# Routing attention with a PReLU FFN on one core: two more pairs of heads in cluster order

## The chip, the cores and the metric

The kernel runs on one core of a Trainium2 chip. The metric is the device time in microseconds of one execution, taken as the median of several runs. TensorE (PE in the profile) multiplies, with its weight loads on a row of their own (PEld); VectorE (DVE), ScalarE (ACT) and GpSimd (POOL) work elementwise; SyncE (SP) only issues transfers, and POOL issues those whose rows are scattered by a list of indices.

## The reference

```python
# q, k, v: (4 batches, 8 heads, 768 tokens, 64); centroids: (8 heads, 16 clusters, 64)
q_assign = argmax(einsum('bhsd,hcd->bhsc', normed(q), normed(centroids)))
k_assign = argmax(einsum('bhsd,hcd->bhsc', normed(k), normed(centroids)))
mask   = q_assign[:, :, :, None] == k_assign[:, :, None, :]
scores = where(mask, q @ k.T / 8, -1e9)
x      = softmax(scores) @ v             # -> (3072 tokens, 512)
h      = x @ w_in                        # 512 -> 2048
g      = maximum(h, 0) + alpha * minimum(h, 0)
out    = g @ w_out                       # 2048 -> 512
```

A query sees only the keys of its own cluster. All products are computed in fp32; the FFN's weights arrive as 64-bit floats and are converted on the chip.

## The kernel before

**Work.** Two heads make a pair `n`; batch `b` has pairs `4b` to `4b+3`, 16 in all. 768 tokens are six tiles of 128, and a half is three tiles (384 columns). In a *full* pair, every half of the queries meets all six chunks of keys: `score` (L757) makes 12 products of 384 columns, ScalarE takes the exponential (L775, L778), VectorE multiplies by the mask (L798), adds up the chunks (L808), transposes and reduces them to row sums (L827, L835), and `weigh` (L893) multiplies by v. `total` (L848) adds the sums across partitions, and `normalise` (L993) writes into `xTs[b, half]`, the FFN's input.

**Pairs in cluster order.** Pairs from `NO` on, 12 to 15, all of batch 3, are treated in another way. Some steps ahead their tokens are ordered by cluster. `load` brings q and k, `order_features` (L562) transposes them into two new tiles, `order_sims` (L573) finds the clusters, `order_counts`, `order_begins` (L598), `order_ranks` and `order_rows` work out each token's row. `order_stage` (L645) loads 256 tokens of q, k and v of one head into one of two stage tiles, three transfers on SP; `order_scatter` (L663) writes 128 rows to a scratch tensor in HBM by an indirect transfer on POOL. A pair has 6 stages and 24 scatters. `order_load` (L669) reads the ordered rows back. Once ordered, a chunk of keys can only match queries in its own tile and the two beside it, so `window(c)` gives each chunk two or three tiles of queries and not six: all of a pair's scores are 12 products, of 256 or 384 columns, and `weigh_near` (L926) has 16, of 128 to 384 columns. `add_near` (L818, L821) adds what lies near. Afterwards the rows go back into their order: `normalise_near` (L932) makes an output tile, `to_rows` (L955) transposes it in two groups of three, ScalarE copies each group to `rows` (L958), `put_back` (L963) scatters it with 12 indirect transfers on POOL, `fetch_back` (L975) reads it with four transfers, and `turn_back` (L985) transposes it into `xTs`, both halves at once.

**Steps and slots.** Everything is emitted in one order written out by hand. `steps` lists three steps for each half of a full pair and three for each pair in cluster order; `UB` = 12 steps make a block. For the first three batches the list runs over halves, pairs and steps, and for batch 3 over pairs and steps:

```python
steps = [(b * NCH + hp, half, s)
         for b in range(WHOLE) for half in range(2)
         for hp in range(NCH) for s in range(SB)]
steps += [(n, None, s) for n in range(NO, NP) for s in range(SB)]
```

From step 24 on (`TOGETHER`) a step has five slots; the first step of a half scores all chunks, and leaves two slots. `later(k, piece)` emits a piece k slots on. `ORDERS` gives the steps at which the four orderings begin; the rest of their times follows from it. `sorting` is a queue of the stages and scatters, from which one piece is emitted in each slot.

**FFN as filler.** The FFN of one half (28 pieces: 16 of four hidden products, L1017; 12 of four output products, L1035) is put in the queue `ffn` when its input is complete, and fed between the attention of the next block, evenly over its slots. `kept(block)` says how many pieces stay in the queue at the end of a block: 4 at the end of the last but one, 12 at the end of the last. These 12 cover the way back of the last pair's rows. The FFN of batch 3 is done at the very end with seven products in place of eight (`last_pieces`, L1195 and L1251).

**Buffers.** `inp` has four tiles for loads, ordered loads, output tiles and fetched rows; `xpool` has two for `xTs`, and one more, `xmore`, holds the second half of batch 3; `ps_m` (`misc`) is one PSUM bank for all small products and the transposes.

Of the kernel before, what the change touches and what calls it, by code (L numbers as in the profile page):

```python
# [19 lines left out]
P = 128  # L20
# [3 lines left out]
def kernel(  # L24
# [79 lines left out]
    pairs = [(b, hp) for b in range(B) for hp in range(NCH)]  # L104
    NO = WHOLE * NCH
    NP = len(pairs)
# [455 lines left out]
    def order_features(n, w):  # L562
        us[n, w] = inp.tile([P, 2, NJ, D], FP32, name="qk").rearrange("p h j d -> p (h j d)")
        nc.vector.transpose(out=us[n, w],
                            in_=raw_qk.pop((n, w)).rearrange("p h j d -> p (h j d)"))

# [11 lines left out]
    def order_counts(n, ps):  # L578

        top, first, pieces = argmax(ps, exact=True)  # L580
        member = sorts["ordp"].tile([P, HS], BF16, name="mine")
        pieces.append(lambda: nc.vector.transpose(
            out=member, in_=top.rearrange("p t c -> p (t c)")))

        def scan():
            count = asg.tile([P, HS], FP32, name="simT")
            nc.vector.tensor_tensor_scan(count, member, member, 0.0, ALU.add, ALU.max)
            us[n] = member, count
        pieces.append(scan)
        for i, piece in enumerate(pieces):  # L590

            later(i if i < len(pieces) - 2 else i + 2, piece) if i else piece()

    def order_begins(n):
# [17 lines left out]
    def order_rows(n, begin, count):  # L612
        ordp, order = sorts["ordp"], sorts["order"]
        by_token = ordp.tile([P, NX, 2, NC], FP32, name="by_token")
        nc.vector.transpose(out=by_token.rearrange("p x h c -> p (x h c)"), in_=count)
        rank = ordp.tile([P, NX, 2], FP32, name="rank")
        nc.vector.tensor_reduce(out=rank, in_=by_token, axis=AX.X, op=ALU.add)
        off = order.tile([P, NX, 2], I32, name="off")
        nc.vector.tensor_scalar(out=off, in0=rank, scalar1=0.0, scalar2=float(2 * S - 1),
                                op0=ALU.max, op1=ALU.min)  # L620
        ranks[n] = off
        whole = tc.dram_tile([2 * 2 * S, P], FP32, name=f"scratch{n}")
        scratch[n] = whole, dram_disjoint_views(whole, 2 * NX)
# [79 lines left out]
    def order_queries(n, h):  # L703
# [225 lines left out]
    def normalise_near(n):  # L929
        outT = inp.tile([P, 2, NJ, D], FP32, name="qk").rearrange("p h j d -> p (h j d)")  # L930
        for side in range(2):
# [5 lines left out]
        found = orders.pop(n)  # L937
        place = sorts["order"].tile([P, 2, NJ], I32, name="place")
        nc.vector.tensor_scalar(out=place, in0=found[:, :, :, 0], scalar1=0, scalar2=S - 1,
                                op0=ALU.max, op1=ALU.min)  # L940
        rows = sorts["byrow"].tile([P, NJ, P], FP32, name="rows")

        starts = (6, 9)
        for i in range(2):
            later(starts[i], lambda i=i: to_rows(outT, rows, i))
            for x in range(NJ):
                later(starts[i] + 2 + x // 2,
                      lambda i=i, x=x: put_back(to, place, rows, i * NJ + x))
        later(starts[1] + 2 + HJ, lambda: fetch_back(n, whole))

    def to_rows(outT, rows, i):

        ps = misc()
        for j in range(HJ):
# [3 lines left out]
        later(1, lambda: nc.scalar.copy(  # L958
            rows[:, i * HJ:(i + 1) * HJ].rearrange("p j d -> p (j d)"), ps[:, 0:HS]))

    def put_back(to, place, rows, i):
# [3 lines left out]
            out_offset=bass.IndirectOffsetOnAxis(ap=place[:, h, j:j + 1], axis=0),  # L965
            in_=rows[:, j, h * D:(h + 1) * D], in_offset=None, element_offset=h * S * D)

    def fetch_back(n, whole):
# [11 lines left out]
        def turn_back():  # L980
            for half in range(2):
                if (b, half) not in xTs:
                    pool = sorts["xmore"] if half else xpool
                    xTs[b, half] = pool.tile([P, NCH, HS], FP32, name="xT")
                nc.vector.transpose(out=xTs[b, half][:, hp, :],  # L985
                                    in_=raw[:, half * HS:(half + 1) * HS])
        later(4 if n == NP - 1 else 9, turn_back)

    def normalise(n, half):
        b, hp = pairs[n]  # L990
        if (b, half) not in xTs:
            xTs[b, half] = xpool.tile([P, NCH, HS], FP32, name="xT")
        nc.vector.tensor_tensor(out=xTs[b, half][:, hp, :],  # L993
                                in0=pos.pop((n, half))[:, 0:HS],
# [98 lines left out]
    def last_pieces():  # L1093
# [195 lines left out]
        def room_for_y():  # L1289
            late.popleft()()  # L1290
            t = xpool.tile([P, NCH, HS], FP32, name="xT").rearrange("p c q -> p (c q)")
            ys.extend(ypool.tile([P, DM], FP32, name="y") for _ in range(HJ))
# [25 lines left out]

    ORDERS = [27, 33, 51, 57]
    prep_at, load_at = {}, {}  # L1320
    for (n, half), u in start_of.items():
        def at(step, slot, piece):
            prep_at.setdefault((step, slot), []).append(piece)
        if half is None:
            t = ORDERS[n - NO]
            load_at.setdefault(t, []).append(lambda n=n: load(n))
            for i in range(2):
                at(t + 2, 2 + 2 * i, lambda n=n, i=i: order_features(n, i))
# [47 lines left out]
    def feed_block(u):  # L1376
        n, half, _ = steps[u - 1]
        if u == NS:
# [4 lines left out]
            return  # L1383
        for i in (range(2) if half is None else (half,)):
            ffn.extend(ffn_pieces(pairs[n][0], i))

    def kept(block):


        return {NS // UB - 2: 4, NS // UB - 1: 12}.get(block, 0)  # L1390

# [55 lines left out]
    for u in range(TOGETHER, NS + 1):  # L1447
# [4 lines left out]
        if s == 0 or u == NS:  # L1452
# [17 lines left out]
            else:  # L1470
                normalise(*prior)
            if u % UB == 0:
                feed_block(u)
                whole = len(ffn) - kept(u // UB)
            if u == NS:
# [21 lines left out]
        else:  # L1497
            slots = range(SLOTS)
        if u == ORDERS[0] - 2:
            order_constants()  # L1500
        for i in slots:
            tick()
            if s == 0:
                prepare(u, FIRST + i - 3)
            at_slot = (u % UB) // SB * FREE + (s * SLOTS + i - 3)
            left = UB // SB * FREE - 1 - at_slot
            pieces = len(ffn) - kept(u // UB) + -whole * left // (UB // SB * FREE)
# [231 lines left out]
```

## Time and profile before

| | us |
|---|---|
| median of 3 runs (963.44 to 963.97) | 963.72 |
| the profiled execution, its own time | 968.97 |
| its span, first to last instruction | 967.2 |
| TensorE busy | 946.1 |
| VectorE busy | 683.5 |
| ScalarE busy | 260.0 |
| POOL busy | 213.2 |

The granted TensorE clock is 1.000 over the whole span. "Busy" of an engine is the time in which at least one of its instructions runs. A group of instructions is named by line, engine and operation, with the tiles it writes and reads, the number of records (an fp32 product leaves two), and the mean length; overlapping instructions count once in the busy time, so that busy time over count is less than the mean.

### The profile page before, as it was taken

What the parts mean: (1) busy time and instruction counts of PE and PEld (TensorE: products, weight loads), DVE (VectorE), ACT (ScalarE), POOL (GpSimd) and SP (SyncE); (2) the same over time, 40 slices, a digit from 0 to 9 for tenths busy, and PEclk for the clock granted to TensorE, in tenths of its full rate; (3) what the DMA queues carried; (4) which work ended last, traced back from release to release, by engine and by line L of the source; (5) the groups of instructions that cost most, each with busy time, mean ns of one, the idle gap of its engine ahead of it and who ended that gap; (6) DMA issues with size and microseconds to landing.
All of it is one profiled execution on the core that took longest, in us unless ns stands there. A gap on an engine that the chain in (4) does not pass through costs nothing.

```text
span 967.2 us, 11202 instructions
## 1 busy us (share of the span) xinstructions
PE 946.1 (98%) x4059; PEld 502.8 (52%) x4059; DVE 683.5 (71%) x1241; ACT 260.0 (27%) x474; POOL 213.2 (22%) x249
## 2 busy tenths in 40 slices
PE   8999999999999999999999999999998999999997
PEld 5534444445454454544545445454454454556886
DVE  5897788798587776977868777678888735598200
ACT  5764533323121231222312223222222210121000
POOL 1432222110000645401000065550043541000000
PEclk9999999999999999999999999999999999999999
DMA  8433666053200463416020031450621112000000
GB/s 290 141 113 102 143 136 118 17 114 88 55 1 22 127 134 70 87 28 123 1 33 1 25 89 50 94 103 11 88 49 30 33 32 56 1 1 0 21 24 25
DMA packets 175583, 64.67 MB, mean 67 GB/s; under 512 B 161360, under 2 KB 165152, under 8 KB 175520
## 3 DMA queue, kind: packets, MB, share of 16 engines
q1 hardware_dynamic: 170064, 55.62, 25.6%
q0 software_dynamic: 4608, 7.87, 2.5%
q8 instruction: 34, 0.56, 0.2%
q10 hardware_dynamic: 848, 0.39, 0.2%
q14 instruction: 29, 0.24, 0.1%
HBM read 45.15 MB, written 18.35 MB: 66 GB/s over the span
## 4 chain that ended last, share of the span: by engine, by line
PE 92%; DVE 5%; issue 1%; ACT 1%; POOL 0%; DVEq 0%; ACTq 0%; POOLq 0%
PE fps L1035 25%; PE fps L1017 25%; PE vps L893 9%; PE sps L757 8%; PE sps L1251 4%; PE sps L1195 4%; PE fps L757 3%; PE vps L1251 2%; PE vps L1195 2%; PE fps L1251 1%; PE fps L1195 1%; PE mps L381 1%; PE mps L926 1%; PE vps L926 1%; PE sps L766 1%
## 5 line engine op out<-in xcount | busy, mean ns | idle before, releaser
L1017 PE MATMUL fps<-xT,w_in_sb 128*128 128x384 f32 x768 | 259.2, 491 | 0.0
L1035 PE MATMUL fps<-w_out_sb,gT 128*128 128x512 f32 x576 | 256.0, 597 | 1.1 <-DVE gT L1009 1.1
L1017 PEld LDWEIGHTS fps<-xT,w_in_sb 128*128 128x128 f32 x768 | 142.3, 190 | 103.9 <-ACT more L778 4.4
L663 POOL DMA_INDIRECT scratch<-stage,off x96 | 102.0, 1063 | 324.8 <-DMA stage<-in_v_dram 269.7
L1035 PEld LDWEIGHTS fps<-w_out_sb,gT 128*128 128x128 f32 x576 | 106.9, 190 | 127.2 <-issue 117.9
L1023 ACT COPY gT<-fps 128x384 f32<-128x384 f32 x96 | 45.9, 478 | 225.0 <-PE fps L1017 212.5
L798 DVE SCALAR_TENSOR_TENSOR more<-aq,key,more 128x384 f32<-128x384 bf16 (+1 forms) x136 | 74.5, 606 | 35.1 <-ACT more L778 20.0
L757 PE MATMUL sps<-qkT 64*128 64x384 f32 (+1 forms) x512 | 97.4, 494 | 0.1
L1009 DVE SCALAR_TENSOR_TENSOR gT<-gT,alpha 128x384 f32<-128x384 f32 x96 | 61.3, 646 | 33.2 <-ACT gT L1023 24.0
L778 ACT ACTIVATE E<-sps 128x768 f32<-128x768 f32 (+1 forms) x81 | 61.0, 801 | 73.2 <-PE sps L766 38.4
L963 POOL DMA_INDIRECT back<-rows,place x48 | 47.7, 994 | 105.1 <-ACT rows L958 91.7
L757 PEld LDWEIGHTS sps<-qkT 64*128 64x128 f32 x512 | 46.3, 186 | 45.0 <-issue 18.1
L798 DVE SCALAR_TENSOR_TENSOR E<-aq,key,E 128x384 f32<-128x384 bf16 (+1 forms) x104 | 56.6, 601 | 17.2 <-ACT E L778 11.3
L893 PE MATMUL vps<-E,vt 128*64 128x384 f32 x356 | 65.7, 494 | 1.5 <-DVE xT L993 1.5
L808 DVE TENSOR_TENSOR acc<-acc,E 128x768 f32<-128x768 f32 x47 | 44.9, 955 | 14.9 <-ACT E L778 13.6
L778 ACT ACTIVATE more<-sps 128x768 f32<-128x768 f32 (+1 forms) x47 | 35.6, 796 | 49.6 <-PE fps L1035 21.6
L893 PEld LDWEIGHTS vps<-E,vt 128*64 128x64 f32 x356 | 23.0, 136 | 33.4 <-issue 31.0
L271 POOL TENSOR_TENSOR w_in_sb<-w_in_sb,power 128x512 f32<-128x512 f32 x16 | 24.3, 1520 | 71.2 <-DVE w_in_sb L268 71.2
L893 PE MATMUL vps<-more,vt 128*64 128x384 f32 x220 | 38.8, 491 | 0.0
L1041 ACT COPY y<-fps 128x512 f32<-128x512 f32 x18 | 10.5, 586 | 100.8 <-PE fps L1035 81.6
L757 PE MATMUL fps<-qkT 64*128 64x384 f32 x160 | 34.9, 508 | 0.6 <-ACT more L775 0.6
L271 POOL TENSOR_TENSOR w_out_sb<-w_out_sb,power 128x512 f32<-128x512 f32 x16 | 22.5, 1410 | 55.8 <-DVE w_out_sb L268 55.8
(282 smaller groups left out, 1074.4 us busy)
## 6 DMA issues: line engine op xcount, KB each, us to landing
raw<-in_moe_w_in_dram SPq DMA_DIRECT2D x16, 512.0 KB
raw<-in_moe_w_out_dram SPq DMA_DIRECT2D x16, 512.0 KB
out_dram<-y SPq DMA_DIRECT2D x21, 256.0 KB
vt<-in_v_dram SPq DMA_DIRECT2D x12, 384.0 KB
qk<-in_q_dram SPq DMA_DIRECT2D x48, 96.0 KB
qk<-in_k_dram SPq DMA_DIRECT2D x48, 96.0 KB
w_in_kept<-w_in_sb SPq DMA_DIRECT2D x8, 512.0 KB
qk<-scratch SPq DMA_DIRECT2D x32, 96.0 KB
```

What stands on the lines that cost most here:

```text
L271: nc.gpsimd.tensor_tensor(out=dst, in0=dst, in1=power[0].bitcast(FP32), op=ALU.mult)
L663: nc.gpsimd.indirect_dma_start(out=scratch[n][1][h * NX + xx], out_offset=bass.IndirectOffsetOnAxis(ap=ranks[n][:, xx, h:h + 1], axis=0), ...
L757: nc.tensor.matmul(out=bank(ps, h, m), lhsT=qkT[r:r + D, S + c * P:S + (c + 1) * P], rhs=qkT[r:r + D, tokens], start=True, stop=not early_ ...
L778: nc.scalar.activation(out=E[:, :, 0:m], in_=ps[:, :, 0:m], func=AF.Exp, scale=SCALE)
L798: nc.vector.scalar_tensor_tensor(out=e, in0=of, scalar=keys[n][:, NJ + c, h:h + 1], in1=e, op0=ALU.is_equal, op1=ALU.mult)
L893: nc.tensor.matmul(out=po[r:r + D, 0:HS], lhsT=vts[n][:, h, c, :], rhs=e[:, h, :], start=(c == 0), stop=(c == NJ - 1))
L963: nc.gpsimd.indirect_dma_start(out=to[i], out_offset=bass.IndirectOffsetOnAxis(ap=place[:, h, j:j + 1], axis=0), in_=rows[:, j, h * D:(h + ...
L1009: nc.vector.scalar_tensor_tensor(out=gs[f], in0=gs[f], scalar=alpha[:, f:f + 1], in1=gs[f], op0=ALU.mult, op1=ALU.max)
L1017: nc.tensor.matmul(out=ps[:, 0:HS], lhsT=w_in_sb[:, c, f * P:(f + 1) * P], rhs=xTs[b, half][:, c, :], start=(c == 0), stop=(c == NCH - 1))
L1035: nc.tensor.matmul(out=ps[:, 0:DM], lhsT=gs[f][:, i * P:(i + 1) * P], rhs=w_out_sb[:, f, :], start=on and f == f0, stop=off and f == f0 + ...
L1195: nc.tensor.matmul(out=bank[to], lhsT=w_in_form(m, x, cc), rhs=rhs[:, cc, :], start=start and cc == 0, stop=cc == KH - 1, skip_group_check ...
L1251: nc.tensor.matmul(out=bank[to], lhsT=g_form(m, x, t), rhs=w_out_form(n, x), start=start and x == 0, stop=x == NQ - 1, skip_group_check=no ...
```

## The change

`NO` becomes 10, so that pairs 10 and 11 of batch 2 go in cluster order too. In batch 2 these two come first, six steps, and then the first halves of pairs 8 and 9, six steps; the second halves of 8 and 9 make a block of six. There are 78 steps and not 84, and blocks start where `begun_at` says: 0, 12, 24, 36, 48, 60, 66. `feeds` says which FFN half is queued at the end of each. `kept` leaves 2, 8 and 12 pieces at steps 60, 66 and 78. Orders begin at six places. A scatter takes a slot of its own, and a stage none. `order_features` transposes in place. Rows of the two halves have a tile each, the two groups of transposes are 6 slots apart and each row transfer has a slot of its own, except for the last pair, which stays as it was but for the two tiles. `xmore` holds the second half of batch 2, and later the results of the last pieces.

```diff
-    NO = WHOLE * NCH
+    NO = WHOLE * NCH - 2
...
     def order_features(n, w):
-        us[n, w] = inp.tile([P, 2, NJ, D], FP32, name="qk").rearrange("p h j d -> p (h j d)")
-        nc.vector.transpose(out=us[n, w],
-                            in_=raw_qk.pop((n, w)).rearrange("p h j d -> p (h j d)"))
+        us[n, w] = raw_qk.pop((n, w)).rearrange("p h j d -> p (h j d)")
+        nc.vector.transpose(out=us[n, w], in_=us[n, w])
...
+        later(len(pieces) + 3, lambda: order_begins(n))
...
-                    sorting.append(lambda i=i - STAGES, x=x: order_scatter(n, i, x))
+                    sorting.append((1, lambda i=i - STAGES, x=x: order_scatter(n, i, x)))
             if i < 2 * PARTS:
-                sorting.append(lambda i=i: order_stage(n, i))
+                sorting.append((0, lambda i=i: order_stage(n, i)))
...
-    steps = [(b * NCH + hp, half, s)
-             for b in range(WHOLE) for half in range(2)
-             for hp in range(NCH) for s in range(SB)]
-    steps += [(n, None, s) for n in range(NO, NP) for s in range(SB)]
+    steps, begun_at, feeds = [], [], {}
+    for b in range(B):
+        whole = [n for n in range(b * NCH, (b + 1) * NCH) if n >= NO]
+        rest = [n for n in range(b * NCH, (b + 1) * NCH) if n < NO]
+        begun_at.append(len(steps))
+        steps += [(n, None, s) for n in whole for s in range(SB)]
+        for half in range(2) if rest else ():
+            if half:
+                begun_at.append(len(steps))
+            steps += [(n, half, s) for n in rest for s in range(SB)]
+            feeds[len(steps)] = b, half
+    begun_at.append(len(steps))
...
-        starts = (6, 9)
+        dense = n == NP - 1
+        starts = (6, 9) if dense else (6, 12)
         for i in range(2):
             later(starts[i], lambda i=i: to_rows(outT, rows, i))
             for x in range(NJ):
-                later(starts[i] + 2 + x // 2,
+                later(starts[i] + 2 + (x // 2 if dense else x),
                       lambda i=i, x=x: put_back(to, place, rows, i * NJ + x))
-        later(starts[1] + 2 + HJ, lambda: fetch_back(n, whole))
+        later(starts[1] + 2 + (HJ if dense else NJ), lambda: fetch_back(n, whole))
...
-    ORDERS = [27, 33, 51, 57]
+    ORDERS = [26, 30, 34, 38, 41, 51]
...
-            at(t + 7, 2, lambda n=n: order_begins(n))
-            load_at.setdefault(u - 4, []).append(lambda n=n: order_load(n))
+            load_at.setdefault(u - (3 if n == NO + 1 else 4), []).append(
+                lambda n=n: order_load(n))
...
-        return {NS // UB - 2: 4, NS // UB - 1: 12}.get(block, 0)
+        return {NS: 12, begun_at[-2]: 8, begun_at[-3]: 2}.get(block_end(u), 0)
...
-            if sorting:
-                sorting.popleft()()
+            while sorting:
+                scatters, piece = sorting.popleft()
+                piece()
+                if scatters:
+                    break
```

More of the change, by code (lines that the diff above doesn't have):

```diff
@@ L937, in normalise_near @@
         found = orders.pop(n)
-        place = sorts["order"].tile([P, 2, NJ], I32, name="place")
-        nc.vector.tensor_scalar(out=place, in0=found[:, :, :, 0], scalar1=0, scalar2=S - 1,
+        place = found[:, :, :, 0]
+        nc.vector.tensor_scalar(out=place, in0=place, scalar1=0, scalar2=S - 1,
                                 op0=ALU.max, op1=ALU.min)
-        rows = sorts["byrow"].tile([P, NJ, P], FP32, name="rows")
-        starts = (6, 9)
+        rows = [sorts["byrow"].tile([P, HJ, P], FP32, name=f"rows{i}") for i in range(2)]
+        dense = n == NP - 1
+        starts = (6, 9) if dense else (6, 12)
         for i in range(2):
@@ L958, in to_rows @@
         later(1, lambda: nc.scalar.copy(
-            rows[:, i * HJ:(i + 1) * HJ].rearrange("p j d -> p (j d)"), ps[:, 0:HS]))
+            rows[i].rearrange("p j d -> p (j d)"), ps[:, 0:HS]))
     def put_back(to, place, rows, i):
@@ L965, in put_back @@
             out_offset=bass.IndirectOffsetOnAxis(ap=place[:, h, j:j + 1], axis=0),
-            in_=rows[:, j, h * D:(h + 1) * D], in_offset=None, element_offset=h * S * D)
+            in_=rows[j // HJ][:, j % HJ, h * D:(h + 1) * D], in_offset=None, element_offset=h * S * D)
     def fetch_back(n, whole):
@@ L981, in turn_back, with x_tile @@
             for half in range(2):
[L982 to L985, printed above, removed]
+                nc.vector.transpose(out=x_tile(b, half)[:, hp, :],
                                     in_=raw[:, half * HS:(half + 1) * HS])
         later(4 if n == NP - 1 else 9, turn_back)
+    def x_tile(b, half):
+        if (b, half) not in xTs:
+            pool = sorts["xmore"] if (b, half) == (WHOLE - 1, 1) else xpool
+            xTs[b, half] = pool.tile([P, NCH, HS], FP32, name="xT")
+        return xTs[b, half]
     def normalise(n, half):
         b, hp = pairs[n]
-        if (b, half) not in xTs:
-            xTs[b, half] = xpool.tile([P, NCH, HS], FP32, name="xT")
-        nc.vector.tensor_tensor(out=xTs[b, half][:, hp, :],
+        nc.vector.tensor_tensor(out=x_tile(b, half)[:, hp, :],
                                 in0=pos.pop((n, half))[:, 0:HS],
@@ L1290, in room_for_y @@
             late.popleft()()
-            t = xpool.tile([P, NCH, HS], FP32, name="xT").rearrange("p c q -> p (c q)")
+            t = sorts["xmore"].tile([P, NCH, HS], FP32, name="xT").rearrange(
+                "p c q -> p (c q)")
             ys.extend(ypool.tile([P, DM], FP32, name="y") for _ in range(HJ))
@@ L1327 @@
             for i in range(2):
-                at(t + 2, 2 + 2 * i, lambda n=n, i=i: order_features(n, i))
+                at(t + 2, 2 + i, lambda n=n, i=i: order_features(n, i))
             at(t + 3, FIRST + 1, lambda n=n: order_sims(n))
-            at(t + 7, 2, lambda n=n: order_begins(n))
-            load_at.setdefault(u - 4, []).append(lambda n=n: order_load(n))
+            load_at.setdefault(u - (3 if n == NO + 1 else 4), []).append(
+                lambda n=n: order_load(n))
             at(u - 4, 0, lambda n=n: prep_clusters(n))
@@ L1376, in feed_block @@
     def feed_block(u):
-        n, half, _ = steps[u - 1]
         if u == NS:
@@ L1383, in feed_block, with kept, block_end, block_start @@
             return
-        for i in (range(2) if half is None else (half,)):
-            ffn.extend(ffn_pieces(pairs[n][0], i))
-    def kept(block):
-        return {NS // UB - 2: 4, NS // UB - 1: 12}.get(block, 0)
+        ffn.extend(ffn_pieces(*feeds[u]))
+    def kept(u):
+        return {NS: 12, begun_at[-2]: 8, begun_at[-3]: 2}.get(block_end(u), 0)
+    def block_end(u):
+        return min(x for x in begun_at if x > u)
+    def block_start(u):
+        return max(x for x in begun_at if x <= u)
     for u in range(-AHEAD, TOGETHER):
@@ L1471 @@
                 normalise(*prior)
-            if u % UB == 0:
+            if u in begun_at:
                 feed_block(u)
-                whole = len(ffn) - kept(u // UB)
+                if u < NS:
+                    whole = len(ffn) - kept(u)
             if u == NS:
@@ L1498 @@
             slots = range(SLOTS)
-        if u == ORDERS[0] - 2:
+        if u == TOGETHER + 1:
             order_constants()
@@ L1504 @@
                 prepare(u, FIRST + i - 3)
-            at_slot = (u % UB) // SB * FREE + (s * SLOTS + i - 3)
-            left = UB // SB * FREE - 1 - at_slot
-            pieces = len(ffn) - kept(u // UB) + -whole * left // (UB // SB * FREE)
+            at_slot = (u - block_start(u)) // SB * FREE + (s * SLOTS + i - 3)
+            room = (block_end(u) - block_start(u)) // SB * FREE
+            pieces = len(ffn) - kept(u) + -whole * (room - 1 - at_slot) // room
             todo.popleft()()
-            if sorting:
-                sorting.popleft()()
+            while sorting:
[3 more added lines that the diff above has]
+                    break
             feed(max(pieces, 0))
```

## The prediction

> **What bounds the kernel now.** I read the page's busy line first, then its chain of waits, then busy time by stage, and last TensorE's timeline in two stages that differ only in how attention is done.
>
> ```profile
> PE 946.1 (98%) x4059; PEld 502.8 (52%) x4059; DVE 683.5 (71%) x1241; ACT 260.0 (27%) x474; POOL 213.2 (22%) x249
> ...
> PE 92%; DVE 5%; issue 1%; ACT 1%; POOL 0%; DVEq 0%; ACTq 0%; POOLq 0%
> ```
>
> TensorE is busy for 946.1 of 967.2 us and carries 92% of the chain that ends last. Whatever takes work off TensorE without opening a gap shortens the run by that work. The 21 us that are not busy lie partly in the first 100 us. The two stages to compare are the block of batch 2's second half (563.88 to 671.60) and the block of batch 3 (671.60 to 777.60); columns are length, then busy time of PE, PEld, DVE, ACT, POOL.
>
> ```profile
> 671.60:777.60 106.00, 99.73 (x441) 51.86 (x442) 83.50 (x151) 26.44 (x53) 35.68 (x36) 1.00 0.27 49
> 563.88:671.60 107.72, 106.58 (x414) 53.10 (x413) 82.70 (x141) 28.35 (x53) 48.89 (x52) 1.00 0.32 69
> ```
>
> The block of full-attention halves loses 1.1 us of TensorE, the block of cluster-ordered pairs 6.3 us. So cluster order is cheap but not free of gaps. TensorE's timeline shows one half of a full pair and, below it, one whole cluster-ordered pair (start, duration, operation):
>
> ```profile
> 563.88 1.56 PE L757 MATMUL sps<-qkT 64*128 64x384 f32 x8
> 565.28 0.81 PE L757 MATMUL fps<-qkT 64*128 64x384 f32 x4
> 566.02 1.51 PE L893 MATMUL vps<-more,vt 128*64 128x384 f32 x8
> 567.36 2.75 PE L893 MATMUL vps<-E,vt 128*64 128x384 f32 x16
> 570.04 0.92 PE L757 MATMUL fps<-qkT 64*128 64x384 f32 x4
> 570.79 1.46 PE L757 MATMUL sps<-qkT 64*128 64x384 f32 x8
> 572.17 0.85 PE L573 MATMUL mps<-qk,cT 128*32 128x384 f32 x8
> ...
> 696.38 1.35 PE L757 MATMUL sps<-qkT 64*128 64x256 f32 x8
> 697.56 0.81 PE L757 MATMUL fps<-qkT 64*128 64x384 f32 x4
> 698.30 1.73 PE L926 MATMUL vps<-E,vt 128*64 128x384 f32 x12
> ...
> 701.91 0.92 PE L757 MATMUL fps<-qkT 64*128 64x384 f32 x4
> 702.66 1.24 PE L757 MATMUL sps<-qkT 64*128 64x384 f32 x8
> 703.83 2.85 PE L1017 MATMUL fps<-xT,w_in_sb 128*128 128x384 f32 x8
> ```
>
> I price by differences of starts, because the durations overlap. A full half: scores 2.14 us (563.88 to 566.02) and 2.13 (570.04 to 572.17), weighted values 4.02 (566.02 to 570.04). A cluster pair needs one such round where a full pair needs two, and each part is smaller: scores 1.92 (696.38 to 698.30) and 1.92 (701.91 to 703.83), values 3.61 (698.30 to 701.91).
>
> **What the skill says.** The Trainium skill, "Perfetto Trace Analysis", section "Identifying the Most-Contended Engine", warns that matmul busy time is no measure of distance to roofline. I therefore check rates: eight hidden-layer products of 384 columns take 5.32 us at 634.02, 0.665 us each, and twelve output products of 512 columns take 10.55 us at 603.63, 0.88 us each: the same 1.7 ns a column, so the FFN filler runs at a steady rate and its busy time is real work. "TensorEngine Tiling (Array Packing)", "Theoretical Speedup", gives up to 2x where a dimension is at most 64. The trace agrees: six score products of 384 columns in 2.14 us are 0.357 us each, 1.86x faster than 0.665. Attention is thus already packed, and what the change saves is at this packed price. "DMA: Bandwidth & Descriptors", "Anatomy of one DMA — SWDGE (gpsimd) path", gives about 2.0 us fixed per DMA from POOL, mostly until the write is confirmed; no view here shows that part for the rows put back, and I use it as an estimate below.
>
> **The change part by part.**
>
> TensorE, two pairs from full to cluster order. Full pair: 2 x (2.14 + 2.13 + 4.02) = 16.58, and two sums of denominators (L848, 560.13 to 560.27) at 0.14: 16.86 us. Cluster pair: 1.92 + 1.92 + 3.61 = 7.45; one wider sum 0.15 (693.49 to 693.64); two groups of three transposes (L955) at 0.33 and 0.38; the two products for the cluster begins (L598, 603.26 to 603.63) 0.37: 8.68 us. The similarities (L381 against L573) and the key spread (L442) are the same for both. Saved: 8.18 us a pair, **16.4 us** in all. The instruction lists confirm the counts: 48 value products of 384 columns fewer against 32 near ones of 128 to 384, 32 score products of 384 fewer and 8 of 256 more, 12 more transposes. The FFN pieces are the same in number; only their places move.
>
> VectorE (rows by operation): 32 fewer masks at 0.61 and 8 more at 0.475, -15.8; 20 fewer adds at 0.954, -19.1; the near adds 2 x 3.6, +7.2; four more transposes before ordering at 0.945, +3.8; the rest of ordering 5.8 a pair, +11.6; queries, turn-back and reciprocals together about +1. Net about -11 us. It is off the path, so I count nothing, but it says that VectorE is no worse off over the span. ScalarE loses about 9 us (12 exponentials fewer at 0.80, 8 at 0.43, against 4 of 512 columns at 0.60 and 4 copies at 0.48).
>
> POOL and SP get more, and this is the cost side. POOL: 48 scatters at 1.063, 24 rows put back at 0.994, 12 copies at 0.2: +77 us, 213 to 290. Its work lies beside TensorE; the scatters feed a load some steps later. SP: 36 more stage loads at 0.61 (576.22 to 577.56), 24 loads from scratch at 0.74 (twelve from 617.22 to 626.15) and 8 fetches at 0.5, less the two loads of v at 0.39: about +43 us of issue. SP waits in its queue for results to store (177 us on L1043), so it has room; those stores, the loads of later pairs and the fetches stand behind each other there.
>
> ```profile
> L663 POOL DMA_INDIRECT scratch<-stage,off x96 | 102.0, 1063 | 324.8 <-DMA stage<-in_v_dram 269.7
> L963 POOL DMA_INDIRECT back<-rows,place x48 | 47.7, 994 | 105.1 <-ACT rows L958 91.7
> ...
> PE mps L955 <- ACT rows L958: 1.9, 2, 1.0
> ```
>
> The pace. One pair's 24 scatters took 555.7 to 594.5, about 39 us. In the new order a pair has 24 slots with room to score, 12 in three steps, so six steps, some 54 us (107.72 / 12 = 9.0 a step): the queue keeps up. The longest chain, pair 15, ends near step 68.4 (loaded at 51, 3 steps to the similarities and some 17 slots to the first scatter, behind pair 14's, which ends at 62.4) and is loaded at 71.
>
> Rows back, pairs 10 and 11. Scatter and put-back now share slots on POOL: 2 x (0.96 + 0.30) = 2.5 us for a slot of 1.8 us, so after 12 slots POOL is up to 8 us late. The turn-back comes 9 slots, 16 us, after the fetch is issued. Needed: 2.0 (the skill's fixed part), and 4.7 from fetch to turn-back (804.12 to 808.80, where VectorE did wait, 4.3 us). 8 + 2 + 4.7 is 14.7 of 16: it just fits, and a few us of waiting are possible. The turn-back is in VectorE's queue, and the masks, slopes and sums of the next half stand behind it; ScalarE's and TensorE's next uses of those tiles wait for them. TensorE covers it at step 60 with the first scores, the values, the second scores and the two FFN pieces now kept for that place: 2.1 + 4.0 + 2.1 + 2 x 3.5 = 15 us. So I cost it at nothing, at most 3 us for both pairs.
>
> Gaps. Of batch 3's 6.3 us, 2.5 (724 to 729) stretch several engines at once without a releaser, and I leave them out; 3.8 us are 0.95 us a pair. Part is the second group of transposes waiting for ScalarE's copy of the first (L955 above, 1.9 us). Two more pairs at that rate: +1.9. Against it: the two groups now start 6 slots apart, not 3, for all but the last pair, and batch 3's block gets 24 FFN pieces instead of 20 (8 carried in, not 4): up to -2 to -3. I take 0, with ends of -3 and +4 for gaps and rows together.
>
> The sum: 967.2 - 16.4 = 950.8 us of span, 968.97 - 16.4 = 952.6 us for the profiled execution. The median of the runs, 963.72, is 5.3 us below that execution; I take the same 16.4 off it: **947.3 us**, -1.7%.
>
> **The rivals.**
>
> A. More is won: batch 3's 3.8 us of gaps close with the extra filler, and the new pairs bring none: 943.5. For it speaks that the full block with dense filler loses 1.1 us; against it, that VectorE still works 79% of that stage (83.5 of 106).
>
> B. VectorE becomes the bound where cluster pairs, two half pairs and an order meet (steps 48 to 60), and late rows hold it: twice batch 3's gap rate, and waits for rows not covered: 5 to 10 us back, 952 to 957. For it: VectorE at 3.9 of 4 us in many short stretches between 704 and 748. Against: its total falls.
>
> C. Slower than before: the scatter chain. Six pairs pass one after another through two stage buffers from step 32 to 68, and put-backs share POOL. Each stage load waits for its buffer's scatters to land. If a pair takes longer than its 54 us, lateness adds up over six pairs; the slack before pair 15's blocks (step 74) is 5.6 steps, 50 us. To lose 16.4 and 1.9 more, the chain must be 68 us late, 11 us a pair, 65 us instead of 39. It would then give 966 or more. The trace's longest waits for a stage inside a pair, 3.7 and 6.1 us, make that unlikely.
>
> That the change does not do what it says is excluded by the instruction counts.
>
> **How the numbers follow.** Likeliest 0.67 (944.5 to 951), A 0.14, B 0.15, C 0.04. Runs of this kernel differ by about 0.2%, 1.9 us, which is what a measurement can tell; every case but C is beyond it. Faster 0.95, same 0.02, slower 0.03 (C's edge gives the 0.02). The range reaches into A and B: 943.5 to 952.5.
>
> **What would show it.** TensorE busy near 930 and not near 946; L926's kind of records 192 instead of 128, the values of full pairs 480 instead of 576; TensorE's idle near 21 us; VectorE near 672, POOL near 290; no releaser on TensorE that is a DMA. Wrong if TensorE's busy time falls by 16 and the span by much less: then VectorE's waits name it, at the turn-back (B) or at the cluster blocks of pairs 14 and 15 (C).

## The result, and the profile after

| | us |
|---|---|
| changed kernel, median of 4 runs (957.46 to 958.22) | 957.55 |
| kernel before, median of 4 runs beside them | 963.58 |
| ratio, with its 95% interval | 0.9939 (0.9922 to 0.9956) |
| the profiled execution, its own time | 958.22 |
| its span | 956.3 |

The change brings 6.0 us, 0.6%, and not the 16.4 us that were forecast. On two of the chips that later runs fell on, TensorE stops now and then, and the kernel before takes 3 to 5 us longer than elsewhere; times from there stand beside the kernel before on the same chip only, and are marked below.

The busy line and the chain by engine, from the page of the changed kernel:

```profile
PE 929.1 (97%) x3995; PEld 496.8 (52%) x3995; DVE 669.4 (70%) x1235; ACT 251.5 (26%) x462; POOL 297.8 (31%) x333
...
PE 77%; DVE 12%; issue 8%; POOL 2%; ACT 1%; DMA 0%; DVEq 0%; POOLq 0%; ACTq 0%
```

TensorE works 17.0 us less than in the first profile of before, as forecast. But its idle time, span less busy, has grown from 21.1 to 27.2 us, and the chain goes over VectorE for 12% where it was 5%. (The share of "issue", 8% where it was 1%, is no guide: e6_sp below has 1% at nearly the same time, e9_orders 8% at 3.5 us less.) The first profile of before had a disturbed stretch (724 to 729 us), so the fair partner is a later profile, that of e8_before below: span 961.7, busy 943.7, idle 18.0. Against it TensorE's work fell by 14.6 us and its idle time rose by **9.2 us**; the difference, 5.4 us, is the gain in span. The busy time of TensorE by stage shows where. First before (second profile), then the changed kernel; columns are length, PE busy, granted clock, share of the DMA engines, GB/s. The stages are: full pairs with orders made beside them; in before both blocks of batch 2, then batch 3; in the changed kernel the two cluster-ordered pairs of batch 2, its full pairs, then batch 3. The limits of before are those of the first profile; in the second one the values of the last pair begin at 769.02 already, so that its last row reaches some 8.6 us into what follows batch 3. Its idle time, 3.4 us, is that of batch 3 all the same: between 769.02 and 777.60 TensorE does not stand still.

```profile
240.00:455.00 215.00, 214.39 (x806) 1.00 0.33 70
455.00:563.88 108.88, 108.88 (x399) 1.00 0.15 25
563.88:671.60 107.72, 106.68 (x420) 1.00 0.31 69
671.60:777.60 106.00, 102.62 (x452) 1.00 0.28 53
```

```profile
240.00:452.00 212.00, 205.38 (x759) 1.00 0.31 73
452.00:512.54 60.54, 57.14 (x242) 1.00 0.57 105
512.54:652.86 140.32, 139.68 (x519) 1.00 0.41 86
652.86:761.91 109.05, 107.19 (x443) 1.00 0.17 35
```

Subtract the second number from the first. The stage with full pairs lost 0.6 us and now loses 6.6. Batch 2 lost 1.0 and now loses 3.4 in its cluster-ordered pairs and 0.6 in the full ones. Batch 3 lost 3.4 and now loses 1.9. That is +6.0, +3.0 and -1.5, together 7.5 of the 9.2 us; 1.7 more lie in the last products, spread over gaps too short to be listed, and were not followed up.

What TensorE waited for is named in the list of waits (who, for what; us in total, times, longest). The lines that concern the small PSUM bank (`mps`), before in the second profile and then after:

```profile
PE mps L955 <- ACT rows L958: 1.9, 2, 1.0
PE mps L848 <- DVE part L835: 1.6, 3, 0.6
PE mps L442 <- ACT rows L958: 0.9, 1, 0.9
PE mps L848 <- ACT gT L1023: 0.5, 1, 0.5
```

```profile
PE mps L856 <- ACT rows L967: 3.6, 5, 1.1
PE mps L856 <- DVE simT L402: 2.7, 3, 1.3
PE mps L442 <- DVE begins L607: 2.2, 2, 1.9
PE mps L856 <- DVE part L843: 1.7, 2, 1.3
...
PE mps L934 <- DVE inverses L869: 1.3, 1, 1.3
...
PE mps L381 <- DVE qk L940: 1.0, 1, 1.0
```

4.9 us have become 12.5 us. Between 240 and 762 us these six lines are all of TensorE's idle time: 6.6 us in the stage with full pairs (2.7 for `simT`, 2.2 for `begins`, 1.7 for `part`), then 3.4, 0.6 and 1.9. In five of the six lines after, what is waited for is not the operand of the product; only `part` is one. The sum of denominators, `total` (L856), does not read `rows` or `simT`: L967 and L402 are the readers of the *previous* content of the bank, and so are L607, L869 and L940 in the other lines. `misc` is a single bank for all small products, so each new product there waits until the last one has been read, and in TensorE's in-order queue all the FFN behind it waits too. The same stretch of TensorE, and then of ScalarE, shows one such wait:

```profile
503.66 1.45 PE L1045 MATMUL fps<-w_out_sb,gT 128*128 128x512 f32 x3
504.95 0.49 PE L964 MATMUL mps<-ident,qk 128*128 128x128 f32 x3
505.28 3.60 PE L1045 MATMUL fps<-w_out_sb,gT 128*128 128x512 f32 x8
509.93 0.42 PE L856 MATMUL mps<-parts,fold 128*128 128x48 f32 x2 [1.06 <-ACT rows L967]
```

```profile
508.91 0.59 ACT L1051 COPY y<-fps 128x512 f32<-128x512 f32 x1 [6.66 <-PE fps L1045]
509.39 0.48 ACT L967 COPY rows<-mps 128x384 f32<-128x384 f32 x1
```

The transposes (L964) fill the bank at 504.95 to 505.44. ScalarE is idle then (for 6.66 us, up to 508.91) and could copy them at once, but ahead of that copy in its queue stands the copy of an FFN result, which TensorE only finishes at 508.9. The rows' copy ends at 509.87; L856, next in the bank, starts at 509.93.

### The profile page after: what moved, and what is told of

It is laid out like the page before. It is cut to its first block, busy times and chain, and to the rows that moved or that the text cites. A ratio compares the mean times of both kernels' runs of the same rounds, so it can differ in the third digit from the quotient of the medians.

```text
span 956.3 us, 11347 instructions
## 1 busy us (share of the span) xinstructions
PE 929.1 (97%) x3995; PEld 496.8 (52%) x3995; DVE 669.4 (70%) x1235; ACT 251.5 (26%) x462; POOL 297.8 (31%) x333
## 4 chain that ended last, share of the span: by engine, by line
PE 77%; DVE 12%; issue 8%; POOL 2%; ACT 1%; DMA 0%; DVEq 0%; POOLq 0%; ACTq 0%
PE fps L1045 23%; PE fps L1027 17%; PE vps L901 7%; PE sps L765 6%; PE sps L1261 4%; PE sps L1205 4%; PE fps L765 2%; PE vps L1261 2%; PE vps L1205 2%; DVE acc L816 1%; PE fps L1261 1%; PE fps L1205 1%; DVE gT L1019 1%; DVE more L806 1%; PE vps L934 1%
## 5 line engine op out<-in xcount | busy, mean ns | idle before, releaser
L663 POOL DMA_INDIRECT scratch<-stage,off x144 | 155.0, 1076 | 222.7 <-DMA stage<-in_v_dram 95.6
L972 POOL DMA_INDIRECT back<-rows,found x72 | 74.3, 1032 | 113.4 <-ACT rows L967 94.0
L765 PE MATMUL sps<-qkT 64*128 64x384 f32 (+1 forms) x480 | 89.2, 490 | 0.0
L806 DVE SCALAR_TENSOR_TENSOR more<-aq,key,more 128x384 f32<-128x384 bf16 (+1 forms) x120 | 65.0, 598 | 19.3 <-ACT more L786 15.7
L765 PEld LDWEIGHTS sps<-qkT 64*128 64x128 f32 x480 | 42.8, 186 | 41.4 <-issue 14.4
L806 DVE SCALAR_TENSOR_TENSOR E<-aq,key,E 128x384 f32<-128x384 bf16 (+1 forms) x96 | 51.6, 595 | 17.7 <-ACT E L786 15.4
L901 PE MATMUL vps<-E,vt 128*64 128x384 f32 x316 | 58.6, 495 | 1.5 <-DVE xT L1003 1.5
L816 DVE TENSOR_TENSOR acc<-acc,E 128x768 f32<-128x768 f32 x37 | 35.2, 952 | 14.7 <-ACT E L786 13.6
L786 ACT ACTIVATE more<-sps 128x768 f32<-128x768 f32 (+1 forms) x42 | 31.4, 783 | 40.6 <-PE sps L765 40.0
L1053 DVE TENSOR_TENSOR y<-y,fps 128x512 f32<-128x512 f32 x24 | 16.4, 683 | 29.8 <-PE fps L1045 29.8
L901 PEld LDWEIGHTS vps<-E,vt 128*64 128x64 f32 x316 | 20.1, 136 | 29.3 <-issue 26.8
```

What stands on the lines that cost most here:

```text
L663: nc.gpsimd.indirect_dma_start(out=scratch[n][1][h * NX + xx], out_offset=bass.IndirectOffsetOnAxis(ap=ranks[n][:, xx, h:h + 1], axis=0), ...
L765: nc.tensor.matmul(out=bank(ps, h, m), lhsT=qkT[r:r + D, S + c * P:S + (c + 1) * P], rhs=qkT[r:r + D, tokens], start=True, stop=not early_ ...
L786: nc.scalar.activation(out=E[:, :, 0:m], in_=ps[:, :, 0:m], func=AF.Exp, scale=SCALE)
L806: nc.vector.scalar_tensor_tensor(out=e, in0=of, scalar=keys[n][:, NJ + c, h:h + 1], in1=e, op0=ALU.is_equal, op1=ALU.mult)
L901: nc.tensor.matmul(out=po[r:r + D, 0:HS], lhsT=vts[n][:, h, c, :], rhs=e[:, h, :], start=(c == 0), stop=(c == NJ - 1))
L972: nc.gpsimd.indirect_dma_start(out=to[i], out_offset=bass.IndirectOffsetOnAxis(ap=place[:, h, j:j + 1], axis=0), in_=rows[j // HJ][:, j % ...
```

## The experiments

**e0_before: the kernel before, profiled again, no edit.**

> The kernel before, profiled a second time. If its first profiled execution was long by accident (968.97 against a median of 963.6), this one shows a span near 962 and no stretch like the one at 724 to 729 us; TensorE's idle outside the first 95 us is then near 7 us and not 10. If instead the first profile was typical, span near 967 and the same gaps.

967.3 us, beside a median of 966.76 of the kernel before on this chip; the stretch at 724 us was there again, smaller. This was one of the chips with stops, which was not known then. It left open whether the stretch belongs to the kernel.

**e1_orders, e2_rows11, e3_both: the bank's users moved apart, first try.** The edits, the third kernel having both:

```diff
-    ORDERS = [26, 30, 34, 38, 41, 51]
+    ORDERS = [25, 30, 34, 37, 40, 51]
```
```diff
-        starts = (6, 9) if dense else (6, 12)
+        starts = (6, 9) if dense else (6, 11)
```

> The changed kernel with three orderings begun a step earlier (25, 37, 40 for 26, 38, 41), so that their similarities and begins no longer stand directly in front of a sum of denominators or a spread of keys in TensorE's queue. Theory of the one small PSUM bank: the five gaps in front of L856 and L442 that VectorE releases (0.74, 0.74, 1.26, 1.89, 0.32 us, together 4.95) go, 957.5 becomes about 952.6. Rival, that VectorE, POOL and the transfers are simply busier in steps 24 to 60: the same work at nearly the same steps, gaps elsewhere, 956.5 to 958.

> The changed kernel with the second group of transposes of the rows one slot earlier (11 for 12 slots after the output). Theory of the one small PSUM bank: ScalarE's copy is then done a slot before the sum of denominators wants the bank; the five gaps in front of L856 that ScalarE's copy releases (1.05, 0.65, 0.62, 0.61, 0.62, together 3.55) go, about 954.0. Rival of a general load: no change, 957 to 958.

> Both edits. Theory of the one small PSUM bank: 8.5 us of gaps go, about 949.0, TensorE busy still 929. Rival of a general load: 956 to 958, with gaps moved to other instructions.

996.46, 988.81 and 1000.53 us, ratios of 1.026 (1.022 to 1.030), 1.022 (1.021 to 1.023) and 1.033 (1.031 to 1.036) to before, on the chip of e0_before. All forecasts missed. The waits that e1 aimed at were gone or smaller (L856 for `simT`: none), but TensorE stopped for up to 13.40 us at a time with no releaser. They could not tell whether the edits or the chip did this.

**e4_after: the changed kernel itself, on another chip.**

> The changed kernel itself, beside the kernel before on the same chip. Theory 1 (the two kernels with moved orders and rows stalled because of what they move): no stretch of several us in which TensorE's records stop without a releaser, a ratio to before of 0.993 to 0.996, TensorE busy 929. Rival (the stalls belong to the chip or the hour of those runs, and the changed kernel has them there too): stretches of 3 to 15 us without a releaser, a clock of 0.5 after them, and a ratio above 1.01. A ratio below 0.99 would speak against both.

957.9 us, ratio 0.9952 (0.9938 to 0.9965), no stops. Two further runs of it on two more chips:

> The changed kernel itself once more. Theory (the stops belong to the chip, and any kernel of this shape has them there): on a chip where the kernel before runs near 967 to 969 us, stops at 485 to 605 us and 985 to 1006 us, a ratio of 1.02 to 1.03; on a chip where it runs near 963, no stops and 957.5, a ratio of 0.994. Rival (the edits bring the stops about, and the changed kernel is free of them): 957 to 961 on either.

> The changed kernel itself. Theory (the stops belong to the chip): where the kernel before runs near 967 to 969 us, stops at 485 to 605 us and 985 to 1006 us; where it runs near 963, none and 957.5. Rival (the changed kernel is free of them): 957 to 961 on either.

957.84 and 958.44 us, 0.9951 (0.9938 to 0.9964) and 0.9948 (0.9931 to 0.9964), no stops; both chips were of the kind where before runs near 963. The gain of 0.5 to 0.6% stands in four sets of runs.

**e5_bank: the bank's users moved apart without moving the transfers.** On the chip of e4_after.

```diff
-            later(starts[i], lambda i=i: to_rows(outT, rows, i))
+            later(min(starts[i], 8), lambda i=i: to_rows(outT, rows, i))
...
-            at(t + 3, FIRST + 1, lambda n=n: order_sims(n))
+            at(t + 3, FIRST + (t % SB < 2), lambda n=n: order_sims(n))
```

> The similarities of the orders that start at steps 26, 38 and 41 are issued one slot earlier, and the second group of transposes of rows is made at slot 8 of 15 and not at slot 12, while the rows go back in the same slots as in the changed kernel. No two users of the one small PSUM bank then follow each other without other matmuls between, and GpSimd's schedule is almost that of the changed kernel. Theory (the bank's previous reader holds TensorE's in-order queue): the waits of the sums of denominators for ScalarE's rows (3.6 us) and for the similarities' reader (2.7 us) and of the key spread for the begins (2.2 us) go, 6 to 8.5 us less than the changed kernel, a ratio to before near 0.986. Rival (VectorE and ScalarE are as late whoever uses the bank, so the waits move to the next matmul that needs them): within 2 us of the changed kernel. If it stalls without a releaser where the changed kernel doesn't, small shifts in time are enough for a stall.

953.63 us, ratio 0.9898 (0.9883 to 0.9913), 4.3 us below e4_after by the medians and 2.9 us by the spans. The bank's waits in e5_bank:

```profile
PE mps L856 <- DVE part L843: 2.3, 2, 1.9
...
PE mps L442 <- DVE begins L607: 1.4, 1, 1.4
PE mps L934 <- DVE inverses L869: 1.3, 1, 1.3
...
PE mps L442 <- ACT rows L967: 1.1, 1, 1.1
PE mps L381 <- DVE qk L940: 1.0, 1, 1.0
PE mps L964 <- ACT rows L967: 0.9, 1, 0.9
...
PE mps L856 <- DVE simT L402: 0.9, 1, 0.9
PE mps L856 <- ACT gT L1033: 0.6, 1, 0.6
```

The five waits of L856 for `rows` (3.6) are gone, those for `simT` fell from 2.7 to 0.9, those of L442 for `begins` from 2.2 to 1.4. In their place L442 and L964 wait for `rows` (2.0), and L856 waits longer for its own operand. 12.5 became 9.5 us, which is the 2.9 us of span: the order of the bank's users is a cause of the lost time, of 3 to 4 us and not of 6 to 8.5.

**e6_sp, e7_two: is it POOL?** e6_sp puts the rows back from SP (`nc.sync.dma_start` in place of the indirect transfer in `put_back`; this leaves out the un-ordering), e7_two emits two scatters a slot. Same chip as e4_after.

> The changed kernel with the rows of the cluster-ordered pairs put back by plain transfers on SyncE's queue, in the order in which they stand (the un-ordering is left out), the same bytes and slots: 72 indirect transfers of about 1 us leave GpSimd, 290 to 298 us down to about 224. Theory (back-to-back indirect transfers of GpSimd hold TensorE up): no stall without a releaser on any chip, at or up to 4 us below the changed kernel. Rival (GpSimd does not matter to TensorE): the same time as the changed kernel within 1.5 us, stalls where that one has them. A third way: SyncE's 36 us more of issue make loads late, and it is slower.

> The changed kernel with two scatters a slot in place of one: the same 216 indirect transfers, in runs that are twice as dense while a pair is scattered. Theory (back-to-back indirect transfers of GpSimd hold TensorE up): more stretches without a releaser than in the changed kernel, 5 us or more slower than it. Rival (their density does not matter): within 1.5 us of the changed kernel; with earlier stage loads it may even be a little faster.

957.0 us, 0.9937 (0.9924 to 0.9951), and 959.24, 0.9961 (0.9948 to 0.9975), against 957.9 for e4_after. POOL's 75 us less are worth 0.9 us, twice the scatters in a slot cost 1.3 us; the intervals overlap with e4_after's. Without any indirect transfer on POOL, and so without the ordering too, beside e14_after and e16_after:

> The changed kernel with every scatter and every row put back as a plain transfer of the same bytes on SyncE's queue, each to the place of its number (the ordering and the un-ordering are left out): no indirect transfer on GpSimd, whose busy time falls from 294 to about 80 us, and some 130 us more of issue on SyncE. Theory (GpSimd's indirect transfers bring the stops about): no stop on a chip where the changed kernel has them. Rival (they do not matter): the same stops, 985 to 1006 us there. On a chip without stops both say 956 to 960, or more if SyncE's queue makes the loads late.

> The changed kernel with every scatter and every row put back as a plain transfer of the same bytes on SyncE's queue (the ordering and the un-ordering are left out). Theory (GpSimd's indirect transfers bring the stops about): no stop where the changed kernel has them, near 960. Rival (they do not matter): the same stops, 985 to 1006 us there. Where the changed kernel has no stop: 957 to 959.

957.7 and 956.1 us, 0.9940 (0.9929 to 0.9952) and 0.9918 (0.9902 to 0.9935): 0.1 and 2.3 us below the changed kernel beside them. By these medians, what POOL got to do explains 0.1 to 2.3 of the 9.2 us, and the waits at the bank stay without it: 12.4 us in e6_sp and e15_noind, 11.9 in e17_noind, where 12.5 stood. The chips had no stops, so what these two were also to tell stays open.

**e8_before: the kernel before once more, on a chip without stops.**

> The kernel before, profiled again. Theory (the stretch at 724 to 729 us, in which TensorE's records come one at a time without a releaser, belongs to the execution that was profiled and not to the median of the runs): on a chip where the runs of the kernel before lie near 963, the stretch is absent, the span is near 961 and TensorE's idle time near 18 us. Rival (the stretch is part of every execution): it is there again and the execution is 3 us or more above the median of the others.

963.47 us, span 961.7, and no stretch at 724 us: from 671.60 to 777.60 TensorE is idle for 3.4 us where it was for 6.3 in the first profile. The first profile's 5.3 us above the median were its own.

**e9_orders: e1 once more, unchanged, on the chip of e8_before.**

> The changed kernel with orders at steps 25, 30, 34, 37, 40 and 51, once more, beside the kernel before. Theory (the long stretches without a releaser belonged to the chip on which it ran): none of them on a chip where the kernel before runs near 963, and a ratio to before of 0.988 to 0.992, since five waits for the small bank are gone. Rival (moved orders bring the stretches about by themselves): a ratio above 1.01 again.

954.38 us, ratio 0.9902 (0.9885 to 0.9918): the program that took 996.46 us. The stops come with the chip and not with the program; that they came with the hour is not excluded, since no chip of these runs served at two times. TensorE in e1_orders, and the same stretch of the program in e9_orders:

```profile
566.27 1.46 PE L765 MATMUL sps<-qkT 64*128 64x384 f32 x8
581.13 4.21 PE L1027 MATMUL fps<-xT,w_in_sb 128*128 128x384 f32 x6 [13.40 <-issue]
```

```profile
544.45 1.46 PE L765 MATMUL sps<-qkT 64*128 64x384 f32 x8
545.84 8.01 PE L1027 MATMUL fps<-xT,w_in_sb 128*128 128x384 f32 x24
```

"issue" says that TensorE waited for nothing that the profile shows. Where nothing stops, the kernel with moved orders, in which L856 never waits for `simT` nor L442 for `begins`, takes 954.4 us, some 3.5 less than the changed one; its waits at the bank are 8.6 us, 3.9 less.

**e10_both and e11_light: what is left of the waits?** Both start from e5_bank. e10_both also moves the orders, e11_light leaves out work of VectorE, the transposes of the features ahead of the orders, so that the order is another one:

```diff
-    ORDERS = [26, 30, 34, 38, 41, 51]
+    ORDERS = [25, 30, 34, 37, 42, 51]
```
```diff
-        nc.vector.transpose(out=us[n, w], in_=us[n, w])
```

> The kernel with the transposes of rows at slots 6 and 8 and the similarities a slot earlier, and now with orders at steps 25, 30, 34, 37, 42 and 51, so that no order's begins or similarities meet the preparation of a pair within 1600 columns before step 60. Theory (small bank and VectorE's local load): of its 11.6 us of gaps after 95 us the waits at 407, 415 and 500 us (1.4, 0.9 and 1.1 us) go, 950 to 952, a ratio near 0.987. Rival (VectorE's local load moves with the orders): within 1 us of it, 953 to 954. Should it stall without a releaser, above 965.

> The kernel with the transposes of rows at slots 6 and 8 and the similarities a slot earlier, with the twelve transposes of the features ahead of the orders left out (the similarities are then taken of untransposed features, and the order is another one): VectorE does 11 us less, TensorE and the transfers the same. Theory (VectorE's local load holds what the small bank's users wait for): the waits in front of the sum of denominators at 285 us and of the key spread and the sum at 407 and 415 us shrink together by 2 us or more, 950 to 951.5. Rival (only the order of the bank's users counts): the same within 1 us.

953.22 us, 0.9894 (0.9878 to 0.9911), and 953.14 us, 0.9889 (0.9873 to 0.9906). In e10_both the waits at 407 and 415 us went, as expected, the one at 500 us (1.1) did not, and L856 waits 2.0 us at 470 instead: the time stays that of e5_bank, as its rival said. In e11_light VectorE has 661.7 us of work where e5_bank has 669.5, and the waits of the bank are the same to 0.1 us, except one of 0.4 us that is gone: its rival holds too. So 7.8 us less of this work on VectorE shorten the waits by 0.4 us at most; the two times are not told apart.

**e13_blocks and e12_all: one neighbour moved, and all edits together.**

```diff
-                    at(u - 7, FIRST + w, lambda n=n, w=w: prep_blocks(n, w))
+                    at(u - (8 if n == NO - 1 else 7), FIRST + w, lambda n=n, w=w: prep_blocks(n, w))
```

> The changed kernel with one edit: the two transposes of queries and keys of batch 2's second full pair are made at step 49 and not at step 50, where VectorE also orders and transposes for the second cluster pair. Theory (VectorE is late at that place by its local load): the waits at 481 us for the reciprocals (1.3 us) and at 487 us for the normalised near values (1.0 us) go or halve, 955.5 to 957. Rival (they wait for the length of the path from scores through the small bank, whoever is late): both stay, 957.3 to 958.3.

> All edits together: transposes of rows at slots 6 and 8, the similarities one slot earlier where the order starts two steps into a pair, orders at steps 27, 30, 34, 37, 40 and 51, and the second full pair's transposes at step 49. Theory (each wait has its own cause, and they add up): the first sum of denominators at 285 us as before (0.6 in place of 1.5 to 1.9), the waits at 407 and 415 us gone, those at 481 and 487 us gone or halved, about 949.5 to 951.5. Rival (VectorE is saturated locally, and what is taken away in one place comes back in another): 953 to 954, as each of the kernels with some of the edits.

1005.61 and 990.46 us, 1.030 (1.024 to 1.036) and 1.023 (1.020 to 1.026), with before at 968.77: the second chip with stops, so neither time answers the question. The wait aimed at, in the changed kernel, and the same place in e13_blocks, ahead of the first stop there (485 us):

```profile
483.17 1.95 PE L934 MATMUL mps<-E,vt 128*64 128x384 f32 x16 [1.30 <-DVE inverses L869]
```

```profile
476.26 0.39 PE L856 MATMUL mps<-parts,fold 128*128 128x48 f32 x2 [1.37 <-ACT gT L1033]
...
482.93 1.90 PE L934 MATMUL mps<-E,vt 128*64 128x384 f32 x16
```

The wait for the reciprocals (1.3 us) is gone, and L856 waits 1.4 us a few us earlier, where it had not waited. The line names ScalarE, but that copy had ended at 475.41; what ended last are the sums that L856 reads, at 476.11 on VectorE (L843), with the moved transposes now ahead of them. The second wait (1.0 us at 487) lies behind the stop in e13_blocks; in e12_all, which has the same edit and no long stop before 515 us, 0.2 us of it are left. But no gain shows there: from the hidden products ahead of L856 to those behind the similarities it takes 16.41 us in e12_all (468.86 to 485.27) and 16.43 in the changed kernel (472.44 to 488.87). In e12_all 1.4 us of it are L856 waiting again, and some 0.7 a halt within L934 whose cause was not found. As far as it can be seen, the waits moved, as the rival of e12_all said. Whether all edits add up was not found out. The best times of kernels that do the whole work are those of e5_bank and e10_both, 953.6 and 953.2 us, 1% below before and not told apart.

## Why the prediction was wrong

**TensorE's saving: right, 1.4 us short by these lines, 1.8 by the whole engine (14.6).** Busy time by line, before (second profile) against after: scores 123.97 and 115.03, -8.9 (forecast -9.4); values, full and near together, 116.42 and 107.63, -8.8 (-8.9); transposes of rows 4.10 and 5.89, +1.8 (+1.4); begins 2.00 and 3.22, +1.2 (+0.7); sums 7.52 and 7.62, +0.1 (-0.3); FFN -0.4 (0). Together -15.0 where -16.4 was forecast. Differences of starts priced the large products well, and the small ones too low: begins and transposes cost 0.9 us more.

**The step that failed: "I take 0, with ends of -3 and +4 for gaps and rows together".** It was +9.2 us. The reading behind it went wrong in three places.

- *The stage.* Gaps were looked for where cluster-ordered pairs are computed. The larger part, 6.0 us, opened where only full pairs run, between 240 and 452 us, where orders are made beside them: its 6.6 us are the three lines of the bank whose wait VectorE ends. Before, two orders began in that stage and it lost 0.6 us; now five do. The step "two more pairs at that rate: +1.9" had taken the rate of one stage for all that a pair brings with it.
- *The wait.* "The two groups now start 6 slots apart, not 3" was counted as a gain. The L955 waits (1.9 us) did go. But the second group came to lie one slot ahead of the sum of denominators, which uses the same bank: five waits of L856 for `rows`, 3.6 us. A step that is moved away from one neighbour was not checked against the next.
- *The credit.* A gain of "up to -2 to -3" was counted for the wider spacing and the denser filler together. Batch 3 lost 1.5 us less: the lines of before there (1.9 for L955, 0.9 for L442, 0.5 for L848) went, and 1.9 us of L856 waiting for `rows` came. What the filler alone did was not tested.

The rows of pairs 10 and 11, the other part of that term, were in time: VectorE waits for fetched rows once, 4.1 us for the last pair, as before, and TensorE for none.

**The 5.3 us between profile and median.** Taking the same 16.4 off both was right: they belonged to the profiled execution (e8_before), and leaving out the stretch at 724 us was right as well. It is for this that the two profiles differ by 10.9 us of span and the medians by 6.0.

**Costed at nothing, and right:** POOL's 85 us and SP's issue (e6_sp, e15_noind, e17_noind: 2.3 us at most, by the medians), and VectorE's and ScalarE's relief (-14.3 and -8.0 us, forecast -11 and -9; that 7.8 us more off VectorE bring nothing is e11_light, for ScalarE no run tests it).

**The rivals.** A did not come: gaps in batch 3 closed by 1.5 of 3.4 us only, and new ones opened. C did not: no wait of TensorE is for a transfer. B, "5 to 10 us back, 952 to 957", gave nearly the size and named VectorE late between steps 48 and 60. In the first six of these steps TensorE lost 3.4 us, 2.3 of them until VectorE was done; the edit aimed at these moved them and showed no gain (e13_blocks, e12_all). The larger part opened before step 48, and what is shown for it is another mechanism, a buffer with one copy and the order of its users: by the order alone 3 to 4 us come back (e5_bank, e9_orders). The cause of the rest of the 9.2 us stays open. In 8.9 of the 12.5 us it is VectorE that is waited for, so its lateness at single places may have a part, though 7.8 us less of its work changed little (e11_light); and no run gave the bank a second copy. The mechanism of the bank stood in the page, as the two waits of L955, and was taken as a detail of two transposes and not as a property of the bank.

## What to carry to other kernels

When work moves in an in-order queue, list every user of each buffer that has one copy, in the new order, and look for two that follow each other closely: the second waits for the reader of the first, which may itself stand behind other work in its queue (L967 above), and all behind the second waits too. Look for the cost of a change in every stage to which it adds instructions, also in those that only prepare; a stage without gaps before is no sign that it can take more. And profile the kernel before twice when a stretch looks disturbed: here 2.5 us of gaps and 5.3 us of time were no part of it.

## What the runs showed of the hardware

**Waits for a bank are mostly waits for its last reader.** The Trainium skill, "PSUM — Partial Sum Buffer", "PSUM bank collisions raise a hardware error", says that two engines must not be in the same bank (and quadrant of partitions) at once and that semaphores have to keep them apart. No run here shows a collision. What the runs show is the waiting where one bank serves all in turn: 10.8 of the 12.5 us in the changed kernel are for a reader of what stood there before. How much of it is due to this rule, and how much to the new product overwriting what is still to be read, they do not tell.

**Stops of TensorE on some chips.** On two chips TensorE stopped for up to 13.4 us, in the longest case with no releaser, at the same places of the program in e1_orders (298.3, 529.8, 567.7 us) and e3_both (298.0, 527.4, 566.9); on the four other chips of these runs, one of them with the program of e1_orders, never. While it stopped, POOL and SP went on. In e1_orders VectorE received the product of L901, whose last records begin at 565.1, only at 577.77:

```profile
577.77 0.56 DVE L1003 TENSOR_TENSOR xT<-vps,rd 128x384 f32<-128x384 f32 x1 [13.70 <-remote]
```

so the records of TensorE seem to stand some 12 us ahead of its results there. "TensorE: Matmul & The Clock Gate", "Part 1: The HAM clock gate", says that the clock halves after an idle window of some 3.4 us; the trace agrees in the halving, with a granted clock of 0.50 between 570 and 586 us of e1_orders (it falls about 2 us after the last record there, about 4 us after it in e3_both) and 0.70 us for a hidden-layer record after the stop (4.21 us for 6) where e9_orders has 0.33 (8.01 for 24). Stops lay in stretches in which POOL issued indirect transfers one behind the other, but e4_after has such stretches without a stop. What starts them was not found, nor whether the changed kernel, which never ran on such a chip, would be slower than before there, as its near copies are by 2 to 3%.
